# Sending the softmax sums of a half chunk to 64 partitions in one transfer, in a four-layer attention kernel with a re-searched order

## The chip, the cores and the metric

The kernel runs on one core of a Trainium2 chip. The metric is the device time of one execution in microseconds (us); the kernel before took 1388.89 us as the median of three runs.

## The reference

The input has 2048 rows of 512 numbers (float32). Four layers follow one another, A, B, A, B, each with 32 heads of 16 numbers:

```
x = x + _A_ref(_layernorm(x), A_wqkv, A_wo)   # each row attends to 8 rows: itself and every second one before it
x = x + _B_ref(_layernorm(x), B_wqkv, B_wo)   # each row attends to itself and the 255 rows before it
x = x + _A_ref(_layernorm(x), A_wqkv, A_wo)
x = x + _B_ref(_layernorm(x), B_wqkv, B_wo)

# in both: q, k, v = split(x @ wqkv); p = softmax(q k^T * 16**-0.5, masked); (p v) reshaped @ wo
```

The change touches the end of the softmax in layer B: there the kernel adds up the exponentials beside the product p v, and divides the product by the sums afterwards.

## The kernel before

**Tiles and stages.** The rows are cut into 8 chunks of 256. Chunk by chunk the kernel runs layer A and then layer B of a pair of layers, so a chunk of layers 0 and 1 is followed by the next chunk of layers 0 and 1, and after 8 chunks come those of layers 2 and 3. Scopes `A0` to `A15` and `B0` to `B15` stand for these 32 chunk layers. TensorE (PE) does the projections with weights split in two float16 halves (L1035 to L1037, L1055 to L1058), the scores of layer B twice (L1421 for the row maximum, L1572 for the exponentials) and p v (L1627). VectorE (DVE) takes the row maximum (L1440, L1436), ScalarE (ACT) the exponential of a wide and a thin piece (L1582 to `p`, L1594 to `ps`), GpSimd (POOL) or DVE masks them (L1611, L1605).

**Who issues transfers.** SyncE (SP) issues most DMAs; ACT issues some between its arithmetic, and while ACT waits to issue one it does nothing else. Every DMA raises one of eight counters, `DMAHW0` to `DMAHW7`, which the program hands out in turn. A DMA that takes a counter again first waits for the earlier transfer on that counter to have landed. In the program before, 389 of ACT's DMA rows and 1240 of SP's carry such a wait.

**What sets the order.** The code calls `plan.add(engine, us, function, r=..., w=..., alt=...)` for each piece of work, a task. `ORDER` holds a number for each task, in the order of the calls: the place of the task in the queue of its engine. A negative number means that the task goes to the engine that `alt` names. `Plan.order` walks through the five queues with the given durations, only to find an order of issue between the engines and to pick PSUM banks. So the sequence on each engine is that of the table, on the chip as in the plan.

**The end of layer B in a chunk.** A chunk has two halves (`hf` 0 and 1, 16 heads each). The tile `os` of a half holds the unnormalized output, 128 partitions by 1024 float32: four groups of 32 partitions, in each group 16 partitions of output and in the next one the sums. What then happens, in 15 of the 16 chunks of layer B (the very last takes another path):

1. `gather` (L1701): the row of sums of each of the four groups goes to 16 partitions of the small tile `rc`, 64 numbers each. That is four DMAs for a half, of 4 KB each.
2. `gather_o` (L1706): the 16 partitions of output of each group go to the tile `oc`, four DMAs of 64 KB for a half.
3. DVE takes the reciprocals of `rc`, 128 partitions by 64 (L1710).
4. One DMA writes them to `scr` in DRAM (L1711), and one reads `scr` back to all partitions of `os` (L1716).
5. POOL or DVE multiplies `oc` by that (L1724), and the output projection follows (`finish`).

Steps 1 and 2 are tasks of SP that may go to ACT. Other names below: `md` and `mt` carry the row maxima (written by L1472, read back by L1478 into `stk_q`), `re` the split queries and keys of a chunk on their way through DRAM (L1345, read back by L1358 and L1360), `sd` the scores of layer A (L1212), `ptd` and `ptt` its weights (L1279, L1286), `vs` its values (L1274).

Of the kernel before, what the change touches and what calls it, by code (L numbers as in the profile page):

```python
# [19 lines left out]
S = 2048  # L20
# [5 lines left out]
W = 8  # L26
# [655 lines left out]
def kernel(  # L682
# [10 lines left out]
    nc = tc.nc  # L693
    layers = "ABAB"
    NL = len(layers)
    plan = Plan()
# [623 lines left out]
    def layer_b(l, c):  # L1320
# [4 lines left out]
        for s in (1, 0):  # L1325
# [23 lines left out]
            for j in range(4):  # L1349
                hf, hp = j // 2, j % 2  # L1350
# [30 lines left out]
        vos = {hf: [Val(os_[hf]), Val(os_[hf])] for hf in range(2)}  # L1381
# [424 lines left out]
```

## Time and profile before

| | |
|---|---|
| three runs | 1382.37, 1388.89, 1390.28 us (median 1388.89) |
| profiled execution | 1382.26 us, of which the span from the first to the last instruction is 1380.5 us |
| PE | busy 1294.3 us (94% of the span) |
| DVE, ACT, POOL | busy 845.2, 823.7, 421.7 us |
| granted TensorE clock | 0.988 of full speed over the span |
| DMA | 195.07 MB, 1664 issues: 1435 by SP, 229 by ACT |

A row of a group of instructions gives how often and how long it ran; rows marked SPq and ACTq are the time of a DMA's issue on that engine's queue, and where such a row holds several issues (x4) it spans the waits between them too. The chain is followed back from the last instruction: each piece is what the next one waited for. In a table of windows the number behind the five engines is the granted clock; 0.50 is half speed.

### The profile page before, as it was taken

How to read it: one execution, taken by the hardware profiler on the slowest of the kernel's cores; microseconds unless marked ns; L12 is line 12 of the kernel's file. 1: busy time of each engine (PE TensorE's matmuls, PEld its weight loads, DVE VectorE, ACT ScalarE, POOL GpSimd, SP SyncE). 2: the span in 40 equal slices, each digit the busy share in tenths (PEclk: the TensorE clock that was granted, in tenths of full speed). 3: DMA queues.
4: the chain of work that ended last, by engine and by line, in shares of the span. 5: the costliest groups of instructions: out<-in, count | busy, mean ns of one | idle time of the engine just before them, and what ended most of it. 6: DMA issues, size and time to landing. Idle time of an engine off the chain costs nothing.

```text
span 1380.5 us, 62387 instructions
## 1 busy us (share of the span) xinstructions
PE 1294.3 (94%) x27206; PEld 835.8 (61%) x27206; DVE 845.2 (61%) x1918; ACT 823.7 (60%) x1302; POOL 421.7 (31%) x881
## 2 busy tenths in 40 slices
PE   9989999998999998999999998989998999998988
PEld 7765556575575655756566564746666575565645
DVE  5565774663747656376664727667483856638594
ACT  8634657565475745756566473848656465653744
POOL 4430203422244332133232141523131251422232
PEclk9999999999999998999999999999999999999999
DMA  8865453735537374464635656374555645444422
GB/s 277 241 152 176 127 126 108 171 104 166 128 106 169 97 188 118 119 168 121 160 104 149 167 140 170 94 205 117 153 113 155 152 120 159 113 124 134 119 74 71
DMA packets 203658, 195.07 MB, mean 141 GB/s; under 512 B 92893, under 2 KB 147933, under 8 KB 203385
## 3 DMA queue, kind: packets, MB, share of 16 engines
q1 hardware_dynamic: 178464, 172.61, 46.2%
q10 hardware_dynamic: 24920, 18.48, 5.2%
q8 instruction: 213, 3.49, 1.1%
q14 instruction: 61, 0.49, 0.1%
HBM read 94.11 MB, written 79.36 MB: 126 GB/s over the span
## 4 chain that ended last, share of the span: by engine, by line
PE 59%; DMA 9%; DVE 8%; ACT 7%; SPq 5%; issue 4%; ACTq 1%; POOL 1%; DVEq 0%; POOLq 0%
PE banks L1627 7%; PE banks L1035 7%; PE banks L1036 6%; PE banks L1037 6%; PE banks L1057 6%; PE banks L1055 6%; PE banks L1058 5%; PE banks L1421 5%; PE banks L1572 5%; DVE m L1436 3%; PE banks L1303 3%; ACT p L1582 2%; PE banks L1194 2%; DMA stk_q<-re 2%; DMA ptt<-ptd 2%
## 5 line engine op out<-in xcount | busy, mean ns | idle before, releaser
L1436 DVE TENSOR_REDUCE m<-banks 128x2 f32<-128x512 f32 x448 | 301.8, 688 | 8.4
L1582 ACT ACTIVATE p<-banks,sclB 128x896 f32<-128x896 f32 x224 | 222.4, 1008 | 95.0 <-PE banks L1572 58.0
L1611 POOL TENSOR_SCALAR_AFFINE_SELECT ps<-ps 64x256 f32<-64x256 f32 x320 | 125.3, 414 | 232.6 <-ACT ps L1594 227.0
L1611 POOL TENSOR_SCALAR_AFFINE_SELECT p<-p 64x256 f32<-64x256 f32 x284 | 111.2, 414 | 265.3 <-ACT p L1582 237.1
L1440 DVE COPY_PREDICATED banks<-trm,banks 128x128 f32<-128x128 int16 x448 | 124.5, 290 | 102.6 <-PE banks L1421 94.8
L1421 PE MATMUL banks<-stk_k,stk_q 48*64 48x320 f16 (+4 forms) x2560 | 137.5, 271 | 25.8 <-DVE m L1436 7.8
L1572 PE MATMUL banks<-stk_q,stk_k 64*64 64x192 f16 (+3 forms) x3584 | 120.8, 238 | 20.7 <-ACT p L1582 5.7
L1421 PEld LDWEIGHTS <-stk_q 48*64 48x64 f16 x2560 | 62.9, 106 | 112.1 <-issue 96.3
L1572 PEld LDWEIGHTS <-stk_k 64*64 64x64 f16 x3584 | 70.7, 107 | 80.6 <-issue 68.6
L1594 ACT ACTIVATE ps<-banks,sclB 128x768 f32<-128x768 f32 x112 | 100.5, 901 | 31.6 <-PE banks L1572 21.0
L1627 PE MATMUL banks<-p,v 64*32 64x192 f32 (+1 forms) x3584 | 111.5, 354 | 5.8 <-ACT s L1203 1.5
L1335 DVE SCALAR_TENSOR_TENSOR el<-banks,eh 128x512 f16<-128x512 f32 x64 | 42.3, 688 | 108.3 <-ACT eh L1332 90.6
L1641 DVE TENSOR_TENSOR os<-os,banks 128x256 f32<-128x256 f32 x112 | 45.5, 415 | 87.7 <-ACT os L1644 82.1
L1644 ACT COPY os<-banks 128x256 f32<-128x256 f32 x112 | 41.3, 373 | 88.4 <-PE banks L1627 72.8
L1203 ACT COPY s<-banks 128x624 f32<-128x624 f32 x64 | 74.9, 1260 | 28.3 <-PE banks L1194 21.7
L1627 PEld LDWEIGHTS banks<-p,v 64*32 64x32 f32 x3584 | 62.3, 106 | 37.7 <-issue 9.5
L1035 PE MATMUL banks<-xh,wA0h 128*128 128x256 f16 x256 | 71.6, 280 | 0.1
L1036 PE MATMUL banks<-xl,wA1h 128*128 128x256 f16 x256 | 70.3, 274 | 1.2 <-DMA xl<-xn 1.2
L1037 PE MATMUL banks<-xh,wA0l 128*128 128x256 f16 x256 | 71.2, 278 | 0.0
L1036 PE MATMUL banks<-xl,wA0h 128*128 128x256 f16 x256 | 71.1, 278 | 0.0
L1035 PE MATMUL banks<-xh,wA1h 128*128 128x256 f16 x256 | 70.8, 277 | 0.0
L1035 PE MATMUL banks<-xh,wB1h 128*128 128x256 f16 x256 | 70.1, 274 | 0.7 <-DVE xl L1019 0.6
(212 smaller groups left out, 3042.3 us busy)
## 6 DMA issues: line engine op xcount, KB each, us to landing
sd<-s SPq DMA_DIRECT2D x96, 156.0 KB
ptt<-ptd SPq DMA_DIRECT2D x128, 96.0 KB
stk_k<-re SPq DMA_DIRECT2D x128, 96.0 KB
stk_q<-re SPq DMA_DIRECT2D x128, 96.0 KB
vs<-vd SPq DMA_DIRECT2D x64, 156.0 KB
re<-eh SPq DMA_DIRECT2D x76, 128.0 KB
vd<-ve SPq DMA_DIRECT2D x32, 256.0 KB
xm<-y SPq DMA_DIRECT2D x32, 256.0 KB
```

The source lines that it names most:

```text
L1035: nc.tensor.matmul(ps[mp].t[:, i], wh, xh, start=k == 0, stop=False)
L1036: nc.tensor.matmul(ps[mp].t[:, i], wh, xl, start=False, stop=False)
L1037: nc.tensor.matmul(ps[mp].t[:, i], wl, xh, start=False, stop=k == 3)
L1055: nc.tensor.matmul(ps.t, xl.t[:, k, tk], wh, start=False, stop=k == 3)
L1421: nc.tensor.matmul(o, lhs, k, start=True, stop=True, tile_position=(64 * par, 64 * h))
L1436: nc.vector.tensor_reduce(out=m.t[:, :, u, qb], in_=ps.t[:, :, 0 : 2 * P], op=ALU.max, axis=AX.X)
L1440: nc.vector.copy_predicated(t[:, :, 0:64], trm[:, 0].bitcast(I16).unsqueeze(1).broadcast_to([P, 2, 64]), t[:, :, C : C + 64])
L1572: nc.tensor.matmul(ps.t[64 * h : 64 * h + 64, par, at + x0 : at + x0 + q1 - q0], stk[hf, kt][r, col, k0 : k0 + 64], stk[hf, 0][r, col, q0: ...
L1582: nc.scalar.activation(big.t[:, 2 * i : 2 * i + 2], ps.t[:, :, 0:448], AF.Exp, scale=scl["B", 1])
L1594: nc.scalar.activation(small.t.rearrange("p (i m) x -> p m i x", i=2), ps.t[:, :, 0:384].rearrange("p m (i x) -> p m i x", i=2), AF.Exp, s ...
L1611: E.affine_select(out=v, in_=v, pattern=[[0, 4], [a, 64]], compare_op=op, fill=0.0, base=0, channel_multiplier=-a)
L1627: nc.tensor.matmul(acc.t[32 * mm : 32 * mm + 32, h, q0:q1], vv[r, 17 * (H * blk + hd) : 17 * (H * blk + hd) + 32], x.t[r, mm, x0 : x0 + q1 ...
```

## The change

The four gathers of a half become one DMA from four partitions to 64, and the reciprocals are written in two DMAs, one for each half, since the rows of `rc` now stand in another order (half, group, piece). All tables of `ORDER` are new; only the numbers in them differ, and two are shown in part. Line numbers of the function move by two up to L1694 (`scores` at L1421 is L1419 in the changed kernel), and `gather` is L1697, `gather_o` L1702, the reciprocals L1706, the write L1710 and the read L1717 there.

```diff
 ORDER = {
-    "S": [0, 8, 1, 2, 10, 3, 16, 9, 7, 15, 14],
...
             def gather(E, hf=hf):
                 s_ = flat(os_[hf])
-                for m in range(4):
-                    s = 16 * (2 * m + hf)
-                    E.dma_start(rc.t[s : s + 16, 0], s_[32 * m + 16 : 32 * m + 17].rearrange("m (k f) -> m k f", f=64))
+                E.dma_start(rc.t[64 * hf : 64 * hf + 64, 0], s_[16::32].rearrange("m (k f) -> m k f", f=64))
...
-            plan.add("SP", 2.6, gather, r=vos[hf], w=[vrc[hf]], size=8, alt=("ACT", 2.7))
+            plan.add("SP", 0.65, gather, r=vos[hf], w=[vrc[hf]], size=8, alt=("ACT", 0.7))
             plan.add("SP", 2.5, gather_o, r=vos[hf], w=[vog[hf]], size=256, alt=("ACT", 2.65))
         plan.add("DVE", 0.47, lambda: nc.vector.reciprocal(rc.t[:, 1], rc.t[:, 0]), r=vrc, w=[vrr])
-        plan.add("SP", 0.4, lambda: nc.sync.dma_start(scr.t.rearrange("m (k f) -> (m k) f", f=64), rc.t[:, 1]), r=[vrr], w=[vscr], size=32)
+
+        def sums_out(E=nc.sync):
+            for hf in range(2):
+                E.dma_start(scr.t[hf::2].rearrange("m (k f) -> m k f", f=64), rc.t[64 * hf : 64 * hf + 64, 1])
+
+        plan.add("SP", 0.8, sums_out, r=[vrr], w=[vscr], size=32)
```

Counted over the program: gathers go from 120 DMAs (84 on SP, 36 on ACT) to 30 (15 and 15), writes of reciprocals from 15 to 30, all on SP. ACT issues 4 more DMAs of `sd`, 4 more of `oc`, 2 more of `ptd`, 2 more of `re`, and 6 fewer of `md`. In all SP issues 1375 DMAs and ACT 214. Work that may run on DVE or POOL moves as well: 13 more masks of `ps` on DVE (32 to 45), 2 fewer of `p` (41 to 39), 4 more subtractions of `xn` (8 to 12), 2 more products of `oc` (5 to 7), one fewer of `ol`; POOL has the opposite change. PE's instructions are the same in number and kind, in another order.

**First place: SP at the end of chunk 1, layer 1.** The order of SP's DMAs behind the row maxima of the last quarter (`md_1_3`), before:

```order
L1472 DMA md_1_3_3667<-mt_1_3_3632 4x32x32 x2
L1701 DMA rc_1_3690<-os_1_0_3055 16x1x64 x4
L1478 DMA stk_q<-md_1_3_3667 2x1024 x2
L1706 DMA oc_1_3775<-os_1_0_3055 16x1024 x4
L1345 DMA re_2_1_3817<-eh_2_1_3791 64x2x512 x3
L1345 DMA re_2_1_3817<-el_2_1_3804 64x2x512
```

and in the changed kernel:

```order
L1702 DMA oc_1_3690<-os_1_0_3063 16x1024 x4
L1132 DMA y_0_0_3738<-xm_0_1439 128x512
L1470 DMA md_1_3_3765<-mt_1_3_3648 4x32x32 x2
L1343 DMA re_2_1_3801<-eh_2_1_3783 64x2x512 x2
L1343 DMA re_2_1_3801<-el_2_1_3792 64x2x512
L1343 DMA re_2_1_3801<-eh_2_1_3783 64x2x512
L1476 DMA stk_q<-md_1_3_3765 2x1024 x2
L1358 DMA stk_k<-re_2_1_3801 48x4x256 x2
```

The gather of the first half is off SP here (it stands on ACT, later, behind the exponentials of quarter 3), and the four DMAs of `oc` stand ahead of the maxima, so that the writes of `re` come directly behind them.

**Second place: ACT at the end of chunk 2, layer 1.** ACT's queue around the transfers of the second half (`os_2_1`), before:

```order
L1250 ACTIVATE l_4_5975<-l_4_5975,sclA_159 128x512
L987 ACTIVATE xn_6_0_6141<-x_6_0_5288,rs_6_5657 128x512
L1370 ACTIVATE v_131<-banks 128x32x16
L1644 COPY os_2_1_5704<-banks 128x256 x2
L1706 DMA oc_2_5407<-os_2_1_5704 16x1024 x4
L1701 DMA rc_2_5467<-os_2_1_5704 16x1x64 x4
L1370 ACTIVATE v_131<-banks 128x32x16
L1472 DMA md_3_0_6299<-mt_3_0_6286 4x32x32 x2
L1166 ACTIVATE qm_5_6328<-banks,half 128x16x32 x4
```

and in the changed kernel:

```order
L1248 ACTIVATE l_4_5899<-l_4_5899,sclA_159 128x512
L1368 ACTIVATE v_131<-banks 128x32x16
L985 ACTIVATE xn_6_0_6119<-x_6_0_4919,rs_6_5516 128x512
L1642 COPY os_2_1_5698<-banks 128x256 x2
L1702 DMA oc_2_5455<-os_2_1_5698 16x1024 x4
L1368 ACTIVATE v_131<-banks 128x32x16
L1470 DMA md_3_0_6292<-mt_3_0_6281 4x32x32 x2
L1277 DMA ptd_143<-bands 64x9x64
L1164 ACTIVATE qm_5_6322<-banks,half 128x16x32 x3
```

The gather is gone from ACT (it is one DMA on SP now, ahead of a write of `vd`), the four DMAs of `oc` stay in front of the second eviction of values to `v`, and a DMA of `ptd` stands two rows behind.

**Third place: ACT at the end of chunk 4, layer 1,** with the counters that each instruction waits for. Before:

```order
L1644 COPY os_4_1_9208<-banks 128x256 [waits DVE_49,PE_49]
L1265 ACTIVATE ve_6_1_9553<-banks 128x512 [waits DMAHW6_49,Activation_49]
L1706 DMA oc_4_8890<-os_4_1_9208 16x1024 [waits DVE_49]
L1706 DMA oc_4_8890<-os_4_1_9208 16x1024 [waits DMAHW0_49]
L1706 DMA oc_4_8890<-os_4_1_9208 16x1024 [waits DMAHW3_49]
L1706 DMA oc_4_8890<-os_4_1_9208 16x1024 [waits DMAHW5_49]
L1701 DMA rc_4_8795<-os_4_1_9208 16x1x64 [waits DMAHW7_49,DMAHW4_49]
L1701 DMA rc_4_8795<-os_4_1_9208 16x1x64 [waits DMAHW0_49]
L1701 DMA rc_4_8795<-os_4_1_9208 16x1x64 [waits DMAHW2_49]
L1701 DMA rc_4_8795<-os_4_1_9208 16x1x64 [waits DMAHW3_49]
L1582 ACTIVATE p_5_1_9648<-banks,sclB_170 128x896 [waits DVE_49,PE_49]
L1594 ACTIVATE ps_5_1_9669<-banks,sclB_170 128x2x2x192 [waits DVE_49,PE_49]
```

and in the changed kernel:

```order
L1277 DMA ptd_143<-bands 64x9x64 [waits DMAHW5_49,DMAHW3_49,DMAHW1_49]
L1642 COPY os_4_1_9192<-banks 128x256 [waits DVE_49,PE_49] x2
L1263 ACTIVATE ve_6_1_9522<-banks 128x512 [waits DMAHW2_49,Activation_49]
L985 ACTIVATE xn_0_1_9544<-x_0_1_8742,rs_0_9010 128x512 [waits DMAHW3_49]
L1697 DMA rc_4_9171<-os_4_1_9192 64x1x64 [waits DMAHW0_49,DVE_49]
L1702 DMA oc_4_8811<-os_4_1_9192 16x1024 [waits DMAHW1_49]
L1702 DMA oc_4_8811<-os_4_1_9192 16x1024 [waits DMAHW4_49]
L1702 DMA oc_4_8811<-os_4_1_9192 16x1024 [waits DMAHW7_49]
L1702 DMA oc_4_8811<-os_4_1_9192 16x1024 [waits DMAHW1_49]
L1592 ACTIVATE ps_5_1_9618<-banks,sclB_170 128x2x2x192 [waits DVE_49,PE_49]
L1580 ACTIVATE p_5_1_9639<-banks,sclB_170 128x896 [waits DVE_49,PE_49]
L1580 ACTIVATE p_5_1_9639<-banks,sclB_170 128x896 [waits PE_49]
```

The single gather now comes ahead of the four DMAs of `oc`, there are three issues fewer between the eviction of `os` and the next exponential, and a normalization (`xn`) and a second DMA of `ptd` have moved in ahead of them.

793 rows, old and new, of the table ORDER are left out of this document.

## Prediction

> **What bounds the kernel now.** I read the page first, then the chain of waits, the rows of the changed lines, the queues of SP and ACT in order of time, and windows around the places found.
>
> ```profile
> span 1380.5 us, 62387 instructions
> PE 1294.3 (94%) x27206; PEld 835.8 (61%) x27206; DVE 845.2 (61%) x1918; ACT 823.7 (60%) x1302; POOL 421.7 (31%) x881
> PE 59%; DMA 9%; DVE 8%; ACT 7%; SPq 5%; issue 4%; ACTq 1%; POOL 1%; DVEq 0%; POOLq 0%
> core 0: 1380.5 us, clock 0.988
> ```
>
> PE is busy for 1294.3 of 1380.5 us, so 86 us are PE's gaps, and the clock of 0.988 costs up to 17 us more (0.012 of the span). Nothing that leaves PE's instructions as they are can win much more than those 103 us; this change moves only what PE waits for. The chain spends 6% in issues of DMAs and 9% in transfers. The question is how much of that belongs to the gathers.
>
> **Price of the issues.** Counts and min/median/max durations in ns:
>
> ```profile
> L1701 SPq DMA_DIRECT2D rc<-os x84: 502/587/1323, 164.3 to 1291.9; - x84
> L1701 ACTq DMA_DIRECT2D rc<-os x36: 510/602/1311, 355.7 to 1317.2; - x36
> L1706 SPq DMA_DIRECT2D oc<-os x88: 498/587/1646, 154.9 to 1319.4; - x88
> L1711 SPq DMA_DIRECT2D scr<-rc x15: 338/349/1774, 196.5 to 1321.0; - x15
> L1472 SPq DMA_DIRECT2D md<-mt x86: 510/564/654, 129.6 to 1349.0; - x86
> ```
>
> A gather of 4 KB and one of 64 KB (L1706) both cost 0.587 us of issue, so the cost doesn't go by bytes; I take 0.59 for the new 16 KB gather to 64 partitions. Before: 84 x 0.587 + 36 x 0.602 = 71.0 us of issue; after: 30 x 0.59 = 17.7. A new write of reciprocals has no row: it leaves the same tile for the same DRAM as L1711 (0.349), but in three dimensions, like L1472 (0.564), to which its shape is nearest. I take 0.564: 30 x 0.564 - 15 x 0.349 = 11.7 us more; with 0.349 it would be 5.2. In all 42 to 48 us of issue time go from two queues, and about 5% of the takers of the eight counters (1664 DMAs become 1589). Most of that was beside PE's work and is worth nothing.
>
> **What of it lies on the path.** In the whole chain the gathers stand in five places, the write of reciprocals in one (first or last pieces of each, with what follows):
>
> ```profile
> 223.36 0.59 SPq L1701
> 225.25 0.60 SPq L1701
> 231.86 3.76 DMA re<-eh
> 356.77 0.53 ACTq L1701
> 357.98 0.60 ACTq L1701
> 358.63 0.61 ACT v L1370
> 443.94 0.59 SPq L1701
> 445.21 0.85 SPq L1701
> 521.48 2.63 DMA rc<-os
> 524.11 1.02 ACT p L1582
> 786.09 0.35 SPq L1711
> 1169.26 0.29 ACTq L1701
> 1171.39 0.60 ACTq L1701
> ```
>
> From start to end that is 2.49 + 1.81 + 2.12 + 2.63 + 2.73 = 11.8 us, the most that the gathers can give back directly. What each gives is bounded by the gap of PE that it ends in:
>
> ```profile
> 240.00:260.00 20.00, 18.74 (x440) 10.61 (x442) 12.97 (x29) 12.57 (x21) 11.50 (x26) 1.00 0.72 197
> 440.00:460.00 20.00, 19.10 (x543) 13.43 (x540) 14.88 (x33) 9.89 (x18) 5.40 (x12) 1.00 0.61 157
> 349.98 5.63 ACTq L1706 DMA_DIRECT2D oc<-os  x4
> 359.28 0.33 PE L1421 MATMUL banks<-stk_k,stk_q 48*64 48x320 f16 x4 [2.53 <-ACT v L1370]
> 354.98:365.22 10.24, 7.71 (x178) 5.01 (x178) 6.06 (x17) 3.13 (x5) 0.00 (x0) 0.83 0.45 105
> 521.48 2.53 ACTq L1701 DMA_DIRECT2D rc<-os  x4
> 525.17 0.48 PE L1421 MATMUL banks<-stk_k,stk_q 48*64 48x320 f16 x4 [1.98 <-ACT p L1582]
> 522.23:535.89 13.66, 11.68 (x239) 5.91 (x231) 7.54 (x16) 7.85 (x11) 4.88 (x12) 0.63 0.53 130
> ```
>
> - *SP at 223* (first place in the order): 2.49 us leave the stretch ahead of the writes of `re`. The loads that wait for those end in 240 to 260, where PE lacks 20 - 18.74 = 1.26 us. I take 1.3; nothing if the read back of `re` is late by itself.
> - *ACT at 356* (second place): the gather leaves ACT. The eviction to `v` then waits for the issues of `oc`, done at 349.98 + 5.63 = 355.61, instead of 358.63, so the gap of 2.53 us can close: 2.5, at the least 0. Late next is whatever the last of the `oc` issues waited for.
> - *SP at 443*: one issue for four, about 1.8 us less, of which PE lacks 20 - 19.10 = 0.9 in 440 to 460: 0.9.
> - *ACT at 521* (third place): three issues fewer ahead of the exponential, 3 x 0.60 = 1.8 of the 1.98 us of gap. The waits of `oc` ahead of them stay.
> - *ACT at 1169*: three issues go (1.8 us), but four of `oc` (2.4 us), which before stood three instructions further on, now come directly behind the gather: 0, between -0.6 and 1.8.
>
> Sum 6.5 us, between 0 and 8.3. SP's second write of reciprocals is on the path once, at 786.09: 2 x 0.564 - 0.35 = 0.8 us more, between 0.3 and 0.8.
>
> The two windows with 0.83 and 0.63 in them show the granted clock: it fell to half behind the gaps at 359 and 525, which costs (1 - 0.83) x 10.24 = 1.7 and (1 - 0.63) x 13.66 = 5.1 us of PE's speed. A shorter gap may keep the clock up or not: 0 to 6.8 us. I take half, 3.4.
>
> **What the new order adds.** ACT gets one task more of `sd` and one more of `oc`, four issues each, 18 instead of 16. The dearest stall of the trace is of that kind, and DVE gets 11 masks and 5 other passes over 128x512 more:
>
> ```profile
> 326.74 7.21 ACTq L1212 DMA_DIRECT2D sd<-s  x4
> 335.10 0.53 PE L1572 MATMUL banks<-stk_q,stk_k 64*64 64x128 f16 x16 [4.37 <-ACT p L1582]
> 327.68:341.33 13.65, 9.28 (x150) 4.31 (x142) 3.38 (x7) 4.61 (x6) 2.93 (x8) 0.75 0.60 179
> L1605 DVE COPY_PREDICATED_SCALAR ps<-trm,nul 128x512 f32 x32 | 25.4, 792 | 11.9 <-ACT ps L1594 11.4 <-ACT mt L1459 0.5
> 60.00:80.00 20.00, 18.58 (x363) 12.85 (x362) 17.34 (x26) 10.48 (x15) 10.21 (x13) 1.00 0.74 186
> 1320.00:1340.00 20.00, 16.58 (x310) 8.00 (x316) 19.55 (x46) 9.90 (x15) 9.50 (x19) 1.00 0.27 75
> ```
>
> At 327 four issues held ACT for 7.21 us; PE lost 4.37 us and (1 - 0.75) x 13.65 = 3.4 us of clock, 7.8 in all. With the stalls at 356 (2.5 + 1.7) and 521 (2.0 + 5.1) that makes 19.1 us over 16 tasks, 1.2 each. Two tasks more would be 2.4; but ACT's issues fall from 229 to 214 as a whole, so I take 1.2, between 0 and 7.8.
>
> DVE's 16 passes at 0.792 us are 12.7 us. DVE is over 17 of 20 us in 8 of 69 windows, of which the first and the last are shown; elsewhere its spare time covers them. I take 12.7 x 8/69 = 1.5 us, between 0 and 12.7. POOL, at 31% busy, loses as much and gains PE nothing.
>
> All tables being new, the rest of the 103 us (90 without the five places and their clock) is dealt again. No row prices that. The three runs of the one program lie 7.9 us apart, so small shifts in time alone move about that much; I take 0, with 8 either way.
>
> **Sum.** 1382.3 (the profiled execution) - 6.5 - 3.4 + 0.8 + 1.2 + 1.5 = 1375.9 us. The profiled execution lies with the fastest of the runs shown, 6.6 below their median; a median of the changed kernel may fall with either, so I add half of that: 1379 us, 0.7% under 1388.89. The ends, all good at once: 1382.3 + 3.3 - 8.3 - 6.8 + 0.3 - 8 = 1363; all bad at once: 1382.3 + 3.3 + 0.8 + 7.8 + 12.7 + 8 = 1415. The second asks for too much; nothing won with one dear stall more is 1382.3 + 3.3 + 0.8 + 7.8 = 1394.
>
> **Rivals.**
>
> *More is won than the five places show.* Eight counters serve all transfers, and 5% fewer take them. If the transfers and issues on the chain (9 + 5 + 1% of the span, 207 us) shrink by the same 5%, that is 10 us more, and with the other half of the clock 3.4: 1366 us. For it speaks that 7.21 us for four issues, where a gather's four take 2.4, are mostly waiting; against it, that most transfers on the chain stand in stretches without a gather.
>
> *Nothing comes of it.* The queue time was covered, and the gaps at 356 and 521 only move to the next wait, on `oc`, which stays on ACT in both places: 1382.3 + 0.8 + 1.2 + 1.5 + 3.3 = 1389 us, no change.
>
> *Slower: DVE.* With 12.7 us more, DVE becomes the one that PE waits for in the stretches where it is full already, as in 1320 to 1340, where PE has 16.58 of 20 us. Each us of gap there costs what it did at 335, (4.37 + 3.4) / 4.37 = 1.78 us: 1379 - 1.5 + 12.7 x 1.78 = 1400 us. It decides (over 1395.8) once more than 10.3 of the 12.7 us fall into such stretches. Against it speak the 61 windows out of 69 with spare time.
>
> *The sums land later.* The new gather leaves four partitions, and `md` is the transfer of before that has four rows on one side:
>
> ```profile
> 783.64 2.38 DMA md<-mt
> 328.47 5.14 DMA stk_k<-re
> POOL oc L1724 <- DMA os<-scr: 50.9, 5, 24.6
>   ACT oh L1105: 1.7, 2
> ```
>
> `md` landed in 2.38 us, no later than the gather's 2.63, and behind the product of `oc` somebody waited only twice (the last row is of those who waited for L1724), 1.7 us. If the two steps of a half (gather and write) took as long as the slowest transfer shown, 5.14, they would be 2 x 2.5 us later; in the two places with a waiter that is 10 us: 1389 us, no change. The Trainium skill (DMA: Bandwidth & Descriptors, "Why a DMA increments its semaphore by 16 and not by 1") says that a transfer is spread over as many of the 16 DMA engines as divides the slowest dimension of both sides; by that rule the new gather and the new writes would run on 4 engines, the old ones on 16. By the rule alone the sum would be this rival's 1389. `md` has 4 by the same rule, and its 2.38 us show no delay.
>
> **How the numbers follow.** A difference under 0.5%, 7 us here, can hardly be told from none. Chances: the forecast (1367 to 1387, centre 1379) 0.42, of which I put 0.31 below 1382 and 0.11 above; more won (1366) 0.20; nothing (1389) 0.20; DVE (1400) 0.13; late sums (1389) 0.05. Faster by over 0.5%: 0.31 + 0.20 = 0.51; within: 0.11 + 0.20 + 0.05 = 0.36; slower: 0.13. The range reaches from 1358, under the 1363 of all good at once by what the first rival would add, to 1398, over the 1394 of one dear stall and short of the slow rival; it leaves out that rival's upper half and a tail of the fast one.
>
> **What would show it.** Right: L1697 with some 0.59 us an issue and 30 of them; L1710 with 30 near 0.56; no gather on the chain for more than 1 us at a place; the gaps of 1.98 us at the end of chunk 4 and of 2.53 us at the end of chunk 2 gone; PE's sum of gaps under 80 us and the clock above 0.99. Wrong: gaps as large at the same ends of chunks, behind `oc` or `sd` on ACT (nothing comes of it), PE waiting for DVE's L1436 more than before (DVE), or `oc` waited for by `oh` (late sums).

## The result, and the profile after

The changed kernel takes 1392.17 us (median of 20 runs, 1386.3 to 1403.46), the kernel before in the same runs 1382.13 us (20 runs, 1372.88 to 1394.94). The ratio is 1.0082, 95% interval [1.0062, 1.0102]: slower by 0.8%. The forecast was 1379 us. 1392 lies in its range, but on the slower side, which had a chance of 0.13.

The profiled execution took 1386.89 us. From its page (span, busy times, chain) and the list of cores:

```profile
span 1385.1 us, 62292 instructions
PE 1293.8 (93%) x27206; PEld 835.8 (60%) x27206; DVE 852.3 (62%) x1925; ACT 827.7 (60%) x1312; POOL 393.8 (28%) x830
PE 59%; DVE 9%; DMA 9%; ACT 8%; issue 3%; SPq 2%; ACTq 1%; POOL 1%; DVEq 0%; POOLq 0%
core 0: 1385.1 us, clock 0.989
```

In this execution TensorE does the same work in the same time as before (1293.8 us against 1294.3) at the same clock, and stands idle for 91.3 us instead of 86.2. It is one of the shortest: third of the 20, and it has the second highest clock, whose mean over the 20 is 0.983. The profiled execution of before, 1382.26 us, lies at its median. So the two profiles show 5 of the 10 us, and part of the rest is clock (below, behind the last run). The chain has lost issue time, as foreseen (SPq 5% to 2%), and the span has not become shorter.

The rows of the tile `rc` (count, min/median/max ns) show the change at work; the last of them is all that anybody waited for it, DVE, twice, 1.8 us together:

```profile
L1710 SPq DMA_DIRECT2D scr<-rc x30: 506/534/616, 193.3 to 1325.8; - x30
L1697 SPq DMA_DIRECT2D rc<-os x15: 578/615/651, 183.3 to 1317.1; - x15
L1697 ACTq DMA_DIRECT2D rc<-os x15: 568/602/792, 184.0 to 1320.2; - x15
  DMA rc<-os: 1.8, 2
```

What TensorE waits for, by line (us in total, times, longest):

```profile
PE banks L1570 <- DMA stk_q<-md: 12.1, 7, 4.8
PE banks L1510 <- DMA stk_q<-md: 5.2, 2, 2.9
PE banks L1419 <- ACT ps L1592: 4.0, 2, 3.6
PE banks L1033 <- ACT v L1368: 3.8, 1, 3.8
```

In the same two places the read back of the row maxima held it for 3.9 and 2.5 us before:

```profile
PE banks L1572 <- DMA stk_q<-md: 3.9, 3, 1.8
PE banks L1512 <- DMA stk_q<-md: 2.5, 2, 2.0
```

The end of chunk 2, where the prediction had placed a gap of 2.53 us that was to close, in order of time:

```profile
343.53 0.37 ACT L1642 COPY os<-banks 128x256 f32<-128x256 f32 x1 [0.65 <-PE banks L1625]
344.68 6.26 ACTq L1702 DMA_DIRECT2D oc<-os  x4
350.99 0.60 ACT L1368 ACTIVATE v<-banks 128x512 f32<-128x512 f32 x1 [7.08 <-DMA oc<-os]
351.63 0.30 PE L1033 MATMUL banks<-xh,wA0h 128*128 128x256 f16 x1 [3.84 <-ACT v L1368]
```

The gather has left the place, and the four writes of `oc` alone now hold ACT for 6.26 us. Added over the rows of TensorE in order of time, gaps (stretches in which it stands idle) of 0.9 us and over come to 45.2 us (24 of them) against 36.1 us (20) before. Five of the 24 stand behind a block of writes on ACT: behind `oc` at 351.6, 769.9 and 1181.0 us (3.8, 1.9, 3.6), behind `sd` at 1069.9 (2.3), behind `re` at 1312.5 (2.2), 13.8 us together.

### The profile page after: what moved, and what is told of

It reads as the page before. It is cut to its first block, busy times and chain, and to the rows that moved or that the text cites. A ratio compares the mean times of both kernels' runs of the same rounds, so it can differ in the third digit from the quotient of the medians.

```text
span 1385.1 us, 62292 instructions
## 1 busy us (share of the span) xinstructions
PE 1293.8 (93%) x27206; PEld 835.8 (60%) x27206; DVE 852.3 (62%) x1925; ACT 827.7 (60%) x1312; POOL 393.8 (28%) x830
## 4 chain that ended last, share of the span: by engine, by line
PE 59%; DVE 9%; DMA 9%; ACT 8%; issue 3%; SPq 2%; ACTq 1%; POOL 1%; DVEq 0%; POOLq 0%
PE banks L1625 8%; PE banks L1033 7%; PE banks L1034 6%; PE banks L1035 6%; PE banks L1055 5%; PE banks L1053 5%; PE banks L1570 5%; PE banks L1056 4%; PE banks L1419 4%; DVE m L1434 3%; PE banks L1301 3%; PE banks L1192 2%; ACT p L1580 2%; DVE banks L1438 2%; DMA stk_q<-re 1%
## 5 line engine op out<-in xcount | busy, mean ns | idle before, releaser
L1434 DVE TENSOR_REDUCE m<-banks 128x2 f32<-128x512 f32 x448 | 302.3, 689 | 8.6
L1609 POOL TENSOR_SCALAR_AFFINE_SELECT p<-p 64x256 f32<-64x256 f32 x292 | 114.8, 415 | 270.1 <-ACT p L1580 265.7
L1419 PE MATMUL banks<-stk_k,stk_q 48*64 48x320 f16 (+4 forms) x2560 | 136.2, 269 | 23.6 <-DMA stk_q<-re 6.7
L1609 POOL TENSOR_SCALAR_AFFINE_SELECT ps<-ps 64x256 f32<-64x256 f32 x268 | 105.9, 418 | 174.0 <-ACT ps L1592 153.3
L1570 PE MATMUL banks<-stk_q,stk_k 64*64 64x192 f16 (+3 forms) x3584 | 120.7, 237 | 24.5 <-DMA stk_q<-md 12.1
L1419 PEld LDWEIGHTS <-stk_q 48*64 48x64 f16 x2560 | 63.2, 105 | 111.3 <-issue 92.4
L1625 PE MATMUL banks<-p,v 64*32 64x192 f32 (+1 forms) x3584 | 114.8, 357 | 6.1 <-ACT p L1580 3.5
L1033 PE MATMUL banks<-xh,wB0h 128*128 128x256 f16 x256 | 70.5, 275 | 0.0
```

Of the source, the lines that this page charges most:

```text
L1033: nc.tensor.matmul(ps[mp].t[:, i], wh, xh, start=k == 0, stop=False)
L1419: nc.tensor.matmul(o, lhs, k, start=True, stop=True, tile_position=(64 * par, 64 * h))
L1434: nc.vector.tensor_reduce(out=m.t[:, :, u, qb], in_=ps.t[:, :, 0 : 2 * P], op=ALU.max, axis=AX.X)
L1570: nc.tensor.matmul(ps.t[64 * h : 64 * h + 64, par, at + x0 : at + x0 + q1 - q0], stk[hf, kt][r, col, k0 : k0 + 64], stk[hf, 0][r, col, q0: ...
L1609: E.affine_select(out=v, in_=v, pattern=[[0, 4], [a, 64]], compare_op=op, fill=0.0, base=0, channel_multiplier=-a)
L1625: nc.tensor.matmul(acc.t[32 * mm : 32 * mm + 32, h, q0:q1], vv[r, 17 * (H * blk + hd) : 17 * (H * blk + hd) + 32], x.t[r, mm, x0 : x0 + q1 ...
```

## The experiments

Two theories stood at first: the new transfers cost more than their issues say (T), or the tables do, being dealt anew (O). Ratios below are to the kernel before, timed beside it on the same chip.

**The two parts of the change apart.** First the tables of before with the new transfers (the diffs are against the changed kernel, where nothing else is said):

```diff
 ORDER = {
-    "S": [0, 16, 3, 11, 21, 1, 10, 4, 2, 15, 14],
+    "S": [0, 8, 1, 2, 10, 3, 16, 9, 7, 15, 14],
...
-            plan.add("SP", 0.65, gather, r=vos[hf], w=[vrc[hf]], size=8, alt=("ACT", 0.7))
+            plan.add("SP", 2.6, gather, r=vos[hf], w=[vrc[hf]], size=8, alt=("ACT", 2.7))
...
-        plan.add("SP", 0.8, sums_out, r=[vrr], w=[vscr], size=32)
+        plan.add("SP", 0.4, sums_out, r=[vrr], w=[vscr], size=32)
```

The two durations are only what the planner reckons with; they are those that go with the old tables, so that every tile also keeps its PSUM bank of before.

> The order of before, with the new transfers in it (one gather DMA for a half instead of four, two writes of reciprocals instead of one); nothing else changes. Theory O (the new order costs the time, the transfers are harmless): no slower than before, between 0 and 8 us faster, since the five gathers on the chain of before shrink. Theory T (the new transfers land late or hold a queue up): about as slow as the changed kernel, 8 to 12 us over before.

Measured: 1360.86 us, 0.9881 [0.9847, 0.9915]. It beats both kernels. Its page:

```profile
span 1360.0 us, 62310 instructions
PE 1289.7 (95%) x27206; PEld 834.2 (61%) x27206; DVE 844.3 (62%) x1918; ACT 823.6 (61%) x1302; POOL 421.0 (31%) x881
PE 61%; DMA 9%; DVE 8%; ACT 7%; issue 3%; SPq 3%; POOL 1%; ACTq 1%; DVEq 0%; POOLq 0%
core 0: 1360.0 us, clock 0.991
```

TensorE's idle time is 70.3 us, 16 less than before, and its gaps of 0.9 us and over come to 20.4 us (15 of them). T is refuted, since it asked for about the time of the changed kernel. Then the reverse, the new tables with four gathers for a half and one write:

```diff
             def gather(E, hf=hf):
                 s_ = flat(os_[hf])
-                E.dma_start(rc.t[64 * hf : 64 * hf + 64, 0], s_[16::32].rearrange("m (k f) -> m k f", f=64))
+                for m in range(4):
+                    s = 16 * (2 * m + hf)
+                    E.dma_start(rc.t[s : s + 16, 0], s_[32 * m + 16 : 32 * m + 17].rearrange("m (k f) -> m k f", f=64))
```

> The order of the changed kernel, with the four gathers and the one write of before. Theory O: as slow as the changed kernel or slower, 10 to 25 us over before, since 40 us of issue time come back into an order made without them. Theory T: about the time of before, within 5 us.

Measured: 1.0296 [1.0255, 1.0337]. Every tile keeps the changed kernel's bank here. The tables cost 3.0% with the old transfers; the transfers are worth 2.1% under the new tables and 1.2% under the old ones. The first of the two kernels, the old order with the new transfers, was timed once more:

> The same kernel as e1 (old tables, new transfers), 0.9881 then, timed again as the base of the parts, which cost 0.0094, 0.0096 and 0.0096 over it where the whole costs 0.0201. If joins between parts cost time of their own it gives 0.988 again; if e1's value was low by chance, 0.990 to 0.992, and the three parts then sum to the whole.

Measured: 0.9895 [0.9855, 0.9936].

**Which tables?** The table gives each task an engine and a place. Counted over the two tables, 260 of the 7,702 tasks have changed engine: 145 among DVE, ACT and POOL, and 115 transfers between the queues of SP and ACT (62 to ACT, 53 to SP). In the next run the 145 go back to their engine of before, each at the rank that the new order gives it; the 115 transfers stay where the new table puts them:

> The changed kernel with its order, but each of the 145 vector tasks that it gives to another engine than before (63 passes from POOL to DVE and 46 back, 14 from ACT to DVE and 22 back) on its engine of before, at its rank in the changed order. Theory A (the deal of tasks to DVE, ACT and POOL costs the 28 us: POOL 393.8 us of work against 421.0, DVE 852.3 against 844.3): at least half comes back, ratio 0.998 or less. Theory O (the order in which tasks stand costs it, whoever does them): 1.004 to 1.012, as the changed kernel, or above, since the order was found for the other deal.

Measured: 1.0142 [1.0114, 1.0171]. POOL had its work back, as its page shows, and nothing was won, so theory A, the deal of work among DVE, ACT and POOL, falls as it was put. By how much the run is slower than the changed kernel says little, since 860 of the 5,632 PSUM tiles also changed bank. The 115 transfers that changed queue were not tested apart from the order: what is called the order below includes them.

```profile
PE 1302.9 (93%) x27206; PEld 837.6 (60%) x27206; DVE 848.5 (61%) x1918; ACT 824.5 (59%) x1302; POOL 422.4 (30%) x881
```

**Where in the program?** The two tables have issued the same tasks after 5,080 of 7,702, and all but one of the same after 2,035, so they can be joined there. `B0`, `B6` and `B13` lie in the three parts; shown is the first joined table against that of the changed kernel:

```diff
     "B0": [75, 76, 78, 79, 33, 34, 35, 80, 224, 82,
...
-    "B6": [503, 504, 509, 511, 157, 158, 159, 514, 1396, 518,
+    "B6": [501, 502, 505, 507, 165, 166, 167, 510, 1390, 513,
...
-    "B13": [1056, 1057, 1062, 1063, 312, 313, 314, 1066, 2843, 1070,
+    "B13": [1055, 1056, 1060, 1061, 326, 327, 328, 1064, 2843, 1067,
```

> New transfers throughout. The table has the changed kernel's engines and order for its first 2,035 of 7,702 tasks (27.8% of TensorE's planned work, into chunk 4's layer 1) and the old engines and order for the rest. The old order with the new transfers gave 0.9881, the new order with them 1.0082: 0.0201, about 28 us, are to be found in three parts. Theory L (the loss stands where TensorE's gaps of 0.7 us and over differ between the two profiled executions: 13.8 us against 7.5 before 390 us, 17.9 against 14.2 up to 930 us, 17.4 against 5.3 after it): this part costs about 6 us, ratio 0.9925. Theory P (the loss is spread evenly over the work): 7.7 us, 0.994. Theory N (the loss is in the join of parts, one late place makes the next): a part alone costs nothing, 0.988, or the three do not sum to 28 us.

> New transfers throughout; the new engines and order for tasks 2,036 to 5,080 alone (27.8% to 66.9% of TensorE's work, where both orders have done the same 5,080 tasks), the old ones ahead of and behind that. Theory L: about 4 us, ratio 0.991. Theory P: 10.9 us, 0.996. Theory N: 0.988, or no sum.

> New transfers throughout; the old engines and order for the first 5,080 tasks, the new ones for the last 2,622. Theory L: about 12 us, ratio 0.997, the dearest part. Theory P: 9.2 us, 0.995. Theory N: 0.988, or no sum.

Measured: 0.9975 [0.9950, 1.0000], 0.9977 [0.9953, 1.0002], 0.9977 [0.9957, 0.9996]. The planner deals out PSUM banks by its own times, and these three were planned with the changed kernel's durations; so the old order was run under those too (this diff is against the first kernel of this section):

```diff
-            plan.add("SP", 2.6, gather, r=vos[hf], w=[vrc[hf]], size=8, alt=("ACT", 2.7))
+            plan.add("SP", 0.65, gather, r=vos[hf], w=[vrc[hf]], size=8, alt=("ACT", 0.7))
...
-        plan.add("SP", 0.4, sums_out, r=[vrr], w=[vscr], size=32)
+        plan.add("SP", 0.8, sums_out, r=[vrr], w=[vscr], size=32)
```

> The old engines and order with the new transfers, as e1, but the planner is given the changed kernel's durations for them (0.65 and 0.8 us for 2.6 and 0.4). The instructions of each engine stand in the same order; the planner hands out the PSUM banks by its own times, so 560 of 5,632 tiles lie in other banks. The three part kernels were planned so, e1 was not. Theory B (the deal of banks carries part of the loss): 0.992 to 1.000, and the parts are to be counted from here. Theory O (the order of the queues alone): 0.988 to 0.990 as e1.

Measured: 0.9900 [0.9868, 0.9931]. In the old order the other banks cost nothing that can be told. The base is then 0.9892, the mean of 0.9881, 0.9895 and 0.9900. Over it each part costs 0.0083 to 0.0085, in all 0.0253, where the whole costs 1.0082 - 0.9892 = 0.0190 (26 us). With intervals of 0.002 to 0.004 on each, that is a loss in all three parts; it isn't one place, and theory N in its first form (a part alone costs nothing) falls. By the times alone L (the loss goes with the gaps that the traces show) and P (it is spread evenly) can't be told apart, and a small price of the joins is not excluded.

The traces say a little more. At the two joins every kernel has run the same matmuls (6,589 and 17,645 records). Windows up to them, of the changed kernel and of the old order with the new transfers (us, TensorE busy, count, clock):

```profile
0.00:373.60 373.60, 351.07 (x6589) 0.99 0.60 163
373.60:910.60 537.00, 506.66 (x11056) 0.99 0.54 142
910.60:1385.10 474.50, 436.10 (x9564) 0.99 0.47 122
```

```profile
0.00:366.70 366.70, 349.25 (x6588) 0.99 0.60 166
366.70:900.70 534.00, 507.51 (x11057) 0.99 0.53 142
900.70:1360.00 459.30, 432.99 (x9564) 1.00 0.47 126
```

The same for the others, one execution each, us:

| | first part | middle | last |
|---|---|---|---|
| before | 377.1 | 539.4 | 464.0 |
| old order, new transfers (three executions) | 366.7, 367.4, 371.6 | 534.0, 538.3, 533.8 | 459.3, 466.3, 464.6 |
| new order in the first part alone | 376.4 | 533.4 | 464.4 |
| in the middle alone | 366.6 | 544.6 | 467.6 |
| in the last alone | 369.0 | 535.7 | 475.1 |
| changed kernel | 373.6 | 537.0 | 474.5 |

In the old order one part varies by 4.5 to 7 us from execution to execution. Beyond that stand the last part, 474.5 and 475.1 against 459.3 to 466.3, and the middle where it was changed alone, 544.6; in that one the clock was 0.97, so part of it is clock.

**Do the waits that the trace names carry it?** The dearest in the sum are those for the maxima. Five of the reads were moved up SP's queue, past transposes and other loads:

```diff
+MOVED = [('B4', 0, 3), ('B7', 0, 3), ('B9', 0, 2), ('B10', 0, 4), ('B11', 0, 3)]
...
+    sp = sorted((t for t in plan.tasks if t.eng == "SP"), key=lambda t: t.place)
+    for scope, j, up in MOVED:
+        t = [t for t in plan.tasks if t.scope == scope and t.fn.__name__ == "mget"][j]
+        i = sp.index(t)
+        sp.insert(i - up, sp.pop(i))
```

> The changed kernel, with five of SP's DMAs moved up: the read back of the row maxima of a chunk's first quarter (md into stk_q; chunks 4 and 7 of layer 1, 1, 2 and 3 of layer 3) stands two to four tasks earlier, ahead of the transposes, copies and gathers that it stood behind. PE waited for these five reads 4.78, 1.70, 1.15, 2.58 and 1.27 us, 11.5 in all, and 5 us more of clock. Theory O1 (the new order costs time because these reads come late): 5 to 12 us faster than the changed kernel, so -2 to +5 us against before. Theory O2 (the loss is spread over many places of the new order): 0 to 3 us faster than the changed kernel, 7 to 10 us over before.

Measured: 1.0094 [1.0060, 1.0128], no gain: of the readings of O, the one by which these reads carry the loss (O1) falls. (350 tiles changed bank in this run; a run below, with these moves and others and all banks held, gave no gain either.) The wait of 12.1 us at the second scores (L1571 here) is no longer among TensorE's first; others stand there:

```profile
PE banks L1420 <- DVE m L1435: 6.3, 17, 0.7
PE banks L1511 <- DMA stk_q<-md: 5.1, 2, 2.7
PE banks L1420 <- DMA stk_q<-re: 4.0, 6, 1.2
PE banks L1571 <- DVE m L1435: 3.9, 9, 0.9
```

Then ACT, one task ahead of each of the five blocks of writes:

```diff
+AHEAD = [(328, 1), (729, 1), (1026, 1), (1126, 1), (1245, 2)]
...
+    act = sorted((t for t in plan.tasks if t.eng == "ACT"), key=lambda t: t.place)
+    for rank, up in AHEAD:
+        act.insert(rank - up, act.pop(rank))
```

> The changed kernel with five moves on ACT's queue: at the five places where its trace shows TensorE waiting (3.8, 1.9, 2.3, 3.6 and 2.2 us, 13.8 in all) for a copy or an exponential that stands on ACT behind a block of writes (four of oc at 351.6, 769.9 and 1181.0 us, four of sd at 1069.9, three of re at 1312.5), that one task goes ahead of the block (of the last block, ahead of two of the three writes). Theory W (the new order loses by the waits that its trace names, each worth its length): about 13 us come back, ratio 0.998 to 1.000. Theory R (a wait taken away at one place comes back as another, as the five reads moved up gave nothing): 1.005 to 1.010, with TensorE's idle time above 80 us.

> The changed kernel with the five moves on ACT and the five reads of maxima moved up on SP (1.0094 alone). Theory W: the ACT moves' 13 us and at most the 12 us that TensorE waits for the maxima, 0.991 to 0.999. Theory R: 1.003 to 1.010.

Measured: 1.0107 [1.0067, 1.0146] and 1.0122 [1.0077, 1.0168]. Since the planner also changed banks in these, two runs made the same moves behind it, with all banks held:

> The changed kernel with the same five moves on ACT as in the run that gave 1.0107, made behind the planner, so that every tile keeps the changed kernel's bank (planned anew, 396 of 5,632 tiles had changed banks). Theory W (the named waits are worth their length, and the new deal of banks had eaten it): 0.997 to 1.002. Theory R (a wait taken away comes back elsewhere, banks or not): 1.005 to 1.010.

> The five moves on ACT and the five reads of maxima moved up on SP, made behind the planner, all banks as in the changed kernel. Theory W: the waits named are worth up to 13 and 10 us, 0.990 to 0.998. Theory R: 1.003 to 1.010.

Measured: 1.0083 [1.0047, 1.0119] and 1.0078 [1.0046, 1.0111]. Still no gain that can be told; banks were not what hid it. The trace of the first of the two shows one way in which a move came to nothing, at the block of `sd`:

```profile
1069.48 0.37 ACT L1643 COPY os<-banks 128x256 f32<-128x256 f32 x1 [1.90 <-PE banks L1626]
1069.55 5.76 ACTq L1211 DMA_DIRECT2D sd<-s  x4
1075.35 0.90 ACT L1593 ACTIVATE ps<-banks,sclB 128x768 f32<-128x768 f32 x1 [5.50 <-DMA sd<-s]
1076.31 0.53 PE L1571 MATMUL banks<-stk_q,stk_k 64*64 64x256 f16 x5 [5.37 <-ACT ps L1593]
```

`os` went ahead, and the exponential behind it now stands behind the block: TensorE waits 5.37 us instead of 2.32. That banks can matter is shown by the new order planned with the old durations:

> The changed kernel with its engines, its order and its transfers, the planner being given the old duration of a gather and of the write (2.6 and 0.4 us): 1,625 of 5,632 tiles lie in other banks, no queue has another order. Theory B (the banks matter): another time than the changed kernel's by over 0.5%, slower since the planner's times fit less, 1.015 to 1.03. Theory O: 1.005 to 1.011.

Measured: 1.0175 [1.0130, 1.0219], 0.9% more than the changed kernel with no queue in another order (besides the banks, 6 of its 1589 transfers take another of the eight counters). So the last run held the banks and moved the blocks far enough, and took the two early reads of maxima along:

```diff
+LATE = [('ACT', 327, 1, 328), ('ACT', 728, 1, 729), ('ACT', 1025, 1, 1030), ('ACT', 1125, 1, 1130), ('ACT', 1243, 2, 1245), ('SP', 86, 1, 87), ('SP', 108, 2, 110),
...
+    for e, first, n, last in LATE:
+        late, t = own[e][first : first + n], own[e][last]
+        a, z = seq.index(late[0]), seq.index(t)
+        seq[a : z + 1] = [x for x in seq[a : z + 1] if x not in late] + late
```

> The changed kernel with all banks kept and every place that its trace shows with a wait of TensorE of 2 us or more taken up in the queues: on ACT the blocks of writes go behind all that TensorE waited for, the sd block behind five tasks and the oc block at 1181 us behind five too (with one task ahead of them, TensorE waited 5.4 and 3.3 us for the next); on SP seven reads of maxima move up, the two at 136 and 173 us among them. The waits so named are 31 us in the changed kernel's trace (12.1 + 5.2 for the maxima, 13.8 behind writes). Theory W: at least half comes back, 0.988 to 0.997. Theory R (the order has no slack to give: what is put later is waited for next): 1.002 to 1.010, TensorE's idle time above 80 us.

Measured: 0.9986 [0.9956, 1.0015]. Neither theory as it was put: 0.0096 of ratio, 13 us, came back, of 31 us of waits named and 26 us of loss. (Behind the moved tasks the counters are dealt anew, and 88 of the 1589 transfers take another; what that is worth was not tested.) Windows as above, and the longest of TensorE's waits now:

```profile
0.00:368.10 368.10, 349.02 (x6589) 0.99 0.61 166
368.10:907.40 539.30, 512.27 (x11056) 0.98 0.53 141
907.40:1383.10 475.70, 436.12 (x9564) 0.98 0.47 121
```

```profile
PE banks L1420 <- DVE m L1435: 8.1, 16, 2.1
PE banks L1302 <- DMA ptt<-ptd: 5.9, 6, 3.1
PE banks L1511 <- DMA stk_q<-md: 5.0, 4, 1.7
PE banks L1420 <- DMA stk_q<-re: 5.0, 6, 2.1
```

In this execution the first part is as short as in the old order (368.1 us). The last is not (475.7): no wait there is longer than 3.1 us, and TensorE's idle time is still 85.7 us over the program.

**How much of it is clock.** In all 17 profiled executions TensorE's busy time multiplied by the granted clock is 1277 to 1281 us (in the changed kernel 1293.8 x 0.989 = 1280; in the run with the old engines, whose clock was 0.981, 1302.9 x 0.981 = 1278): the work is the same, and it takes longer in proportion as the clock is lower. So the span and the clock of any run give an estimate of both shares: 1279 / clock - 1279 is lost to the clock, and the span less 1279 / clock is idle time. Means over the runs whose clock is on record:

| | runs | span, us | clock | idle, us (estimate) | clock, us (estimate) |
|---|---|---|---|---|---|
| before | 83 | 1380.7 | 0.985 | 83 | 19 |
| old order, new transfers (three kernels) | 18 | 1363.6 | 0.990 | 72 | 13 |
| changed kernel | 20 | 1391.4 | 0.983 | 90 | 22 |
| all long waits moved | 12 | 1382.1 | 0.987 | 87 | 16 |

By this the new order costs some 19 us of idle time and 9 us of clock. What the last run won back is more clock (6 us) than idle time (4 us): the clock is higher with the long waits gone, and most of the idle time is still there.

So it is shown that the transfers gain about 1.1% (15 us) and that the new tables, by the order of the tasks and the queues of the 115 transfers, take 1.9% (26 us); that this stands in all parts of the program; and that moving tasks at a dozen places, where a queue has a block of writes, or of loads, ahead of what TensorE needs next, gives about half of it back. What takes the other half stays open; by the windows of single executions most of it stands in the last third. No experiment put a single wait of the old order into the new one there, and none changed the order without the queues.

## Why the prediction was wrong

*The step that failed* is the last ahead of the sum: "All tables being new, the rest of the 103 us [...] is dealt again. No row prices that. [...] I take 0, with 8 either way." The new tables as a whole stood in the sum with 2.7 us (1.2 for ACT's tasks, 1.5 for DVE's, 0 for this) and cost 26, about two thirds of it idle time and one third clock by the estimate above. So this term, even with the 2.7 us taken off, was some 23 us, nearly three times its bound. The 8 us were taken from the spread of the runs of one program, and that says how far small shifts of time move one order, not how far two orders lie apart. No row of before gives the 26; but between the two tables 22 to 34% of the neighbours in each queue have changed places, and 8 us was too narrow for that. Which waits make up the second half of the 26 us stays open.

*The gathers* were counted at 6.5 us, with 3.4 of clock. The runs under the old order give 15 us for the transfers as a whole, against 9.1 in the sum (6.5 + 3.4 - 0.8). The direction was right and the size too small: the single places on the chain gave too little. The rival that more is won (1366 us) has the time that the transfers alone gave, since 0.9892 of 1382 is 1367 us; that its reason holds, 5% less of all transfers and issues on the chain, is not shown: on the chain there SPq fell from 5% to 3%, while DMA stayed at 9%. TensorE's gaps of 0.9 us and over fell from 36.1 to 20.4 us in that order, in places that the chain had not named too: the gap of 4.37 us behind `sd` at 335 became 2.12.

*Issue prices*: 0.59 and 0.564 us were forecast for a gather and a write, 0.602 to 0.615 and 0.534 measured, 30 of each. Right. No gather stands on the chain for more than 0.62 us.

*The gaps at the ends of chunks 2 and 4* were to close. At chunk 2 it grew to 3.84 us behind `oc`, which the prediction had named as the sign of failure; at chunk 4 it went, but one of 4.78 us for the maxima of that chunk came at 436 us.

*ACT's two tasks more* were priced at 1.2 us, between 0 and 7.8. Blocks of writes on ACT stand ahead of 13.8 us of gaps in the changed kernel. Two more blocks, 18 instead of 16, can hardly give that by their number; the rows above show what matters, namely which task stands directly behind a block and whether TensorE needs it.

*DVE* was priced at 1.5 us, and the slow rival rested on it. TensorE's wait for L1434 at the first scores is 6.4 us, 7.8 before for the same line; with the old engines the new order was slower still. That rival named the right direction (1400 us) for a reason that this wait and that run speak against.

*The base.* Half of 6.6 us, 3.3, was added because three runs of before had a median of 1388.89. Over 20 runs its median is 1382.13 us, that of the profiled execution, so there was nothing to add.

*Late sums*: not seen. Under the old order with the new transfers nobody waited for the tile `rc`, and in the changed kernel DVE did, twice, for 1.8 us; there `oh` waited once, for 0.8 us, for the product of `oc`, against twice and 1.7 us before. The Trainium skill (DMA: Bandwidth & Descriptors, "Why a DMA increments its semaphore by 16 and not by 1") would have the new gather on 4 of 16 DMA engines. No run here shows on how many it was; a cost of it isn't seen, since the kernel with these transfers and the old order is the fastest.

*The signs*: idle time of TensorE 91.3 us and clock 0.989, where under 80 and over 0.99 were named as right. The old order with the new transfers had 70.3 and 0.991.

## What to carry to other kernels

When a change comes with a new schedule, time the two apart before pricing either: here a gain of 1.1% lay under a loss of 1.9%. The order of a tuned kernel can be worth more than the edit that it comes with, and the spread between the runs of one order is no measure of what another order costs. A named wait's length was no measure of what its removal gave here: moves at 13.8 us of named waits gave nothing while the block only passed one task, and moves at 31 us, with the blocks behind every task that the waiting engine needed, gave 13; look at what comes next behind the block before moving one task ahead of it. And one profiled execution may be one of the shortest of its kernel: compare its clock with that of the other runs before reading a difference of 5 us from two profiles.

## What the runs showed of the hardware

The time that four writes of the same size hold a queue is no constant. Under the old order with the new transfers, ACT's blocks of four writes of `oc` took from 2.6 to 6.5 us from the first issue to the last, the waits between them included, in rows of this kind:

```profile
501.44 6.49 ACTq L1704 DMA_DIRECT2D oc<-os  x4
686.72 2.56 ACTq L1704 DMA_DIRECT2D oc<-os  x4
```

A single issue of `oc` on ACT has a median of 0.600 us there. Nearly all of ACT's transfers may have to wait for a counter first. In the kernel before, of the 389 rows with such a wait that are named ahead of the prediction as ACT's DMAs, 212 are DMAs (of 229), and 177 are other instructions of ACT.

TensorE's long waits mostly go with a lower clock, and then cost more than their length. Of the changed kernel's eight gaps of 2.2 us and over seven lie in a window of 10 us with a lower granted clock, for example those of 2.88, 3.84 and 4.78 us (us, TensorE busy, count, clock):

```profile
130.00:140.00 10.00, 7.12 (x55) 0.84 0.49 141
350.00:360.00 10.00, 8.37 (x104) 0.83 0.46 122
430.00:440.00 10.00, 5.21 (x88) 0.68 0.61 90
```

At 0.83 that is 1.7 us of TensorE's speed, at 0.68 it is 3.2. Of the 16 gaps from 0.9 to 2.2 us one had such a window, the next one behind it. The length of a gap is no rule, though: under the old order with the new transfers, where no gap is longer than 2.12 us, one of 1.78 us at 834 has a window as low:

```profile
830.00:840.00 10.00, 7.94 (x185) 0.72 0.66 186
```

Over the program these two profiled executions lose (1 - 0.989) x 1385.1 = 15 us and (1 - 0.991) x 1360.0 = 12 us to the clock; over all runs of the two orders it is some 22 and 13, as estimated above.
